# A planner that accounts for the way to SBUF shared by POOL and VectorE, and early chunks whose low parts are formed from PSUM

## The chip, the cores and the metric

The kernel runs on one core of a Trainium2 chip. The metric is the device time of one execution in microseconds (us). The five engines of the core are named as the profile names them: PE is TensorE (PEld its weight loads), DVE is VectorE, ACT is ScalarE, POOL is GpSimd, and SP issues the transfers. About 0.2% is what repeated runs of this kernel differ by.

## What is computed

A convolution-like attention over 2 x 4096 positions of width 192, followed by two feed-forward layers of inner width 2048. The first feed-forward applies h cos(h), the second a leaky ReLU.

```python
def _attn_ref(x, weight_gen):                 # (2,4096,192), (2,4096,8,7)
    w = weight_gen - np.max(weight_gen, axis=-1, keepdims=True)
    w = np.exp(w)
    w = w / (np.sum(w, axis=-1, keepdims=True) + 1e-09)
    x_pad = np.concatenate([np.zeros((B, K - 1, D), dtype=np.float32), x], axis=1)
    idx = np.arange(S)[:, None] + np.arange(K)[None, :]
    x_unf = x_pad[:, idx, :].reshape(B, S, K, H, D // H)
    return np.einsum('bshk,bskhg->bshg', w, x_unf).reshape(B, S, D)

def _moe_ref(x, w_in, w_out):                 # (8192,192), (192,2048), (2048,192)
    h = x @ w_in
    return ((h * np.cos(h)) @ w_out).astype(np.float32)

def _moe2_ref(x, w_in, w_out):
    h = x @ w_in
    return (np.maximum(0.01 * h, h) @ w_out).astype(np.float32)

def reference(**kwargs):
    x = _attn_ref(x, weight_gen).reshape(8192, 192)
    return _moe2_ref(_moe_ref(x, moe_w_in, moe_w_out), moe2_w_in, moe2_w_out)
```

The feed-forward weights arrive as 64-bit floats.

## The kernel before

**Tiles and chunks.** The 8192 tokens are cut into 16 blocks b of 512. For each layer m (0 and 1) and block, the inner width is cut into 16 pieces f of 128. One (m, b, f) is a chunk; there are 512. A chunk is five matmuls of 512 columns into a PSUM bank `h` (L645: the product is split into high and low float parts, three with the first 128 input rows, two with the remaining 64), then the activation, then the activated tile as a high part `hi` and a low part `lo`, then five matmuls that add into the block's accumulators: three with `hi` (L694 to L696) and two with `lo` (L699, L700). For m = 0 the activation is: turns on ACT (L657), angle on DVE (L664), sine on ACT (L669), product on DVE (L672), all into an SBUF tile `g`; then `hi` by a copy on ACT (or DVE) and `lo = g - hi` on POOL (L235). For m = 1 ACT applies the leaky ReLU in place in PSUM (L681) and copies `hi`, and DVE forms `lo = h - hi` from PSUM (L235).

**Streams.** Two streams of chunks alternate; the second starts six chunks later. `pos` numbers the chunks in this sequence. The first 34 contain 32 chunks of m = 0 and two of m = 1.

**Attention.** Blocks 0 and 1 form seven products of 128x768 on DVE (L461) and PE sums them through an identity (L466). Blocks 2 to 15 form products (L392, first one L385) and sums (L399, L407, L414) on DVE, all from SBUF to SBUF.

**Weights.** In the first 190 us eight groups of weights (m, g) are loaded and converted from 64-bit pieces: `size`, `low` on ACT (L564, L585), `clamp` on POOL (L567), `shift` and `merge` on DVE (L572, L578), `add` on POOL (L590), then a high copy on ACT or DVE (L230, L232) and a low subtraction on POOL (L235).

**The plan.** Nothing of the order is written by hand. Each operation is given to `Plan.op` with a due time (in chunks), a cost for each engine that may do it, what it reads and writes, and its buffers. `Plan.emit` keeps a clock for each engine, and again and again takes the operation that can start first: among those of an engine that can start within `NEAR` of the first, the one with the smallest due time. An engine other than an operation's first one is taken only where the first is busy (`ELSE`, `LEAVE`). A cost written as a tuple marks a DVE operation with SBUF operands only. Before the change such a cost is multiplied by `SHARED` = 1.55 if POOL is busy at that moment; POOL's own start doesn't depend on DVE. PE operations are held to start `SLACK` = 0.5 us after what they need, whichever engine made it.

**Buffers that matter here.** `h` takes one of three banks, `g` one of five tiles, `hi` and `lo` one of four each. A buffer comes free when its last user ends.

## Time and profile before

| | before |
|---|---|
| median of 3 runs | 1287.84 us (1287.0 to 1288.92) |
| profiled execution | 1289.18 us, its span 1287.2 us |
| PE busy in the span | 1233.0 us, 96% |
| DVE, ACT, POOL busy | 933.4 (73%), 883.4 (69%), 489.0 (38%) |
| mean granted PE clock | 0.989 of full speed |

A row's busy time includes what it waits for inside, for instance for a way to memory. PE's matmuls overlap: one row lasts about 0.39 us where a new one starts every 0.23 us, so PE's pace is read from starts and counts.

### The profile page before, as it was taken

How to read it: one execution, taken by the hardware profiler on the slowest of the kernel's cores; microseconds unless marked ns; L12 is line 12 of the kernel's file. 1: busy time of each engine (PE TensorE's matmuls, PEld its weight loads, DVE VectorE, ACT ScalarE, POOL GpSimd, SP SyncE). 2: the span in 40 equal slices, each digit the busy share in tenths (PEclk: the TensorE clock that was granted, in tenths of full speed). 3: DMA queues.
4: the chain of work that ended last, by engine and by line, in shares of the span. 5: the costliest groups of instructions: out<-in, count | busy, mean ns of one | idle time of the engine just before them, and what ended most of it. 6: DMA issues, size and time to landing. Idle time of an engine off the chain costs nothing.

```text
span 1287.2 us, 15419 instructions
## 1 busy us (share of the span) xinstructions
PE 1233.0 (96%) x5416; PEld 995.6 (77%) x5416; DVE 933.4 (73%) x1343; ACT 883.4 (69%) x1642; POOL 489.0 (38%) x398
## 2 busy tenths in 40 slices
PE   5798799999999999999999999999999999999998
PEld 4576587777778878787788878788787877888886
DVE  7998998889875776849795595866869586554333
ACT  4688776787776766767676666667676676776654
POOL 5898872566332322323323232322323232232000
...
GB/s 162 79 127 52 143 72 13 58 32 1 1 1 44 1 15 29 1 58 1 43 1 2 43 1 44 1 51 1 1 44 1 44 1 13 1 1 13 1 13 25
DMA packets 15037, 39.50 MB, mean 31 GB/s; under 512 B 1781, under 2 KB 8307, under 8 KB 14961
## 3 DMA queue, kind: packets, MB, share of 16 engines
...
q8 instruction: 42, 0.69, 0.2%
q14 instruction: 35, 0.28, 0.1%
...
## 4 chain that ended last, share of the span: by engine, by line
PE 58%; DVE 28%; ACT 7%; issue 4%; POOL 1%; DMA 1%; SPq 0%; ACTq 0%; DVEq 0%; POOLq 0%
PE h L645 29%; DVE pr L392 5%; DVE g L672 4%; DVE g L664 4%; PE acc1r L696 3%; PE acc1m L700 3%; PE acc1m L694 3%; PE acc1m L695 3%; PE acc1r L699 3%; PE acc0m L694 3%; DVE xa L399 3%; PE acc0r L696 3%; PE acc0m L695 3%; DVE lo L235 3%; PE acc0r L699 2%
## 5 line engine op out<-in xcount | busy, mean ns | idle before, releaser
L235 POOL TENSOR_TENSOR lo<-g,hi 128x512 fp32r<-128x512 f32 x256 | 358.6, 1402 | 622.1 <-ACT hi L230 552.9
L235 DVE TENSOR_TENSOR lo<-h,hi 128x512 fp32r<-128x512 f32 x256 | 175.5, 687 | 167.5 <-ACT hi L230 165.0
L669 ACT ACTIVATE g<-g 128x512 f32<-128x512 f32 x256 | 161.5, 631 | 146.5 <-DVE g L664 145.9
L672 DVE TENSOR_TENSOR g<-h,g 128x512 f32<-128x512 f32 x256 | 175.1, 687 | 82.9 <-ACT g L669 81.5
L664 DVE SCALAR_TENSOR_TENSOR g<-g,h 128x512 f32<-128x512 int32 x256 | 173.8, 681 | 56.6 <-ACT g L657 55.0
L681 ACT ACTIVATE h<-h 128x512 f32<-128x512 f32 x256 | 149.0, 582 | 86.2 <-PE h L645 85.6
L657 ACT ACTIVATE g<-h 128x512 int32<-128x512 f32 x256 | 151.2, 591 | 61.0 <-PE h L645 60.0
L230 ACT ACTIVATE hi<-g 128x512 fp32r<-128x512 f32 x242 | 152.0, 630 | 36.2 <-DVE g L672 34.2
L230 ACT ACTIVATE hi<-h 128x512 fp32r<-128x512 f32 x256 | 151.4, 592 | 6.5 <-PE acc1r L696 0.2
L694 PE MATMUL acc0m<-hi,ohi 128*128 128x512 f32 x256 | 105.0, 410 | 16.5 <-ACT hi L230 14.9
L645 PE MATMUL h<-x0hi,ihi 128*128 128x512 f32 x256 | 102.4, 400 | 4.1 <-DVE g L672 2.7
L699 PE MATMUL acc0r<-lo,or 128*128 128x512 f32 x256 | 102.4, 400 | 3.0 <-POOL lo L235 3.0
L699 PE MATMUL acc1r<-lo,or 128*128 128x512 f32 x256 | 100.6, 393 | 3.7 <-DVE lo L235 3.6
L694 PE MATMUL acc1m<-hi,ohi 128*128 128x512 f32 x256 | 102.5, 400 | 0.1
L645 PE MATMUL h<-x1hi,ihi 128*128 128x512 f32 x256 | 101.8, 398 | 0.8 <-DVE g L672 0.8
L645 PE MATMUL h<-x0rh,r 128*128 128x512 f32 x256 | 101.0, 395 | 1.1 <-ACT x0rh L230 1.1
L695 PE MATMUL acc1m<-hi,olo 128*128 128x512 f32 x256 | 100.1, 391 | 1.8 <-POOL olo L235 1.8
L645 PE MATMUL h<-x1hi,ilo 128*128 128x512 f32 x256 | 100.5, 393 | 1.4 <-POOL ilo L235 1.4
L645 PE MATMUL h<-x0lo,ihi 128*128 128x512 f32 x256 | 100.6, 393 | 0.7 <-DVE x0lo L235 0.7
L645 PE MATMUL h<-x0hi,ilo 128*128 128x512 f32 x256 | 100.8, 394 | 0.0
L645 PE MATMUL h<-x0rl,r 128*128 128x512 f32 x256 | 100.6, 393 | 0.0
L645 PE MATMUL h<-x1rl,r 128*128 128x512 f32 x256 | 100.3, 392 | 0.1
...
## 6 DMA issues: line engine op xcount, KB each, us to landing
...
```

Of the source, the lines that this page charges most:

```text
L230: nc.scalar.activation(out=out, in_=in_, func=AF.Copy)
L235: eng[e].tensor_tensor(out=out, in0=a, in1=b.bitcast(F32), op=ALU.subtract)
L645: nc.tensor.matmul(h(), w[:, c], v(), start=i == 0, stop=i == len(terms) - 1)
L657: nc.scalar.activation(out=k, in_=h(), func=AF.Copy, scale=0.5 / math.pi, bias=0.25)
L664: nc.vector.scalar_tensor_tensor(out=g(), in0=g().bitcast(I32), scalar=-2 * math.pi, in1=h(), op0=ALU.mult, op1=ALU.add)
L669: nc.scalar.activation(out=g(), in_=g(), func=AF.Sin, bias=math.pi / 2)
L672: nc.vector.tensor_tensor(out=g(), in0=h(), in1=g(), op=ALU.mult)
L681: op(pos + 0.6, {"ACT": 0.58}, lambda e: nc.scalar.activation(out=h(), in_=h(), func=AF.Prelu, alpha=0.01), [kh], [kg], [h])
L694: nc.tensor.matmul(am(), ohi[:, f % GF, :], ghi(), start=first, stop=False)
L695: nc.tensor.matmul(am(), olo[:, f % GF, :], ghi(), start=False, stop=False)
L696: nc.tensor.matmul(ar(), orr[:, f % GF, :], ghi(), start=first, stop=False)
L699: nc.tensor.matmul(ar(), orr[:, f % GF, :], glo(), start=False, stop=last)
```

## The change

1. **The planner's clock for the shared way.** A variable `port` holds the time until which either a POOL operation or a DVE operation with a tuple cost runs. Either kind may start only after it. `SHARED` goes. If a POOL and such a DVE operation could start within `YIELD` of each other, the one with the earlier due time goes.
2. **Costs.** The costs of most operations on DVE and POOL are new numbers; more DVE operations are marked as tuples.
3. **Choice and slack.** `NEAR` is 0.6 and each us of delay counts as 20 chunks of due time. What PE needs from PE itself has no slack any more; what others need from PE counts 0.06 + 0.17 us.
4. **Chunks kept in PSUM.** For odd `pos` below 34 and m = 0 the product is written back into the bank `h`; `hi` is copied from there (ACT or DVE), and `lo = h - hi` is formed by DVE instead of POOL. The bank is held until then.
5. **Offers.** Turns of m = 0, copies `hi` of m = 1, and the weights' `size` and `low` may also go to DVE.

```diff
-    HOP = 0.08
+    HOP = 0.06
     SLACK = 0.5
-    NEAR = 0.12
+    NEAR = 0.6
+    IDLE = 20.0
...
-    SHARED = 1.55
+    DRAIN = 0.17
+    YIELD = 0.01
...
-            t = max(o.ready + (self.SLACK if e == "PE" else 0.0), free[e], wire - 2.0 if e == "SP" else 0.0)
+            t = max(o.ready, free[e])
+            if e == "PE":
+                t = max(t, o.ready + self.SLACK if o.ready else 0.0)
+            else:
+                t = max(t, o.own)
...
+            if e == "POOL" or isinstance(o.cost[e], tuple):
+                t = max(t, port)
...
-                    t, _, o = min((a for a in at if a[0] <= t0 + self.NEAR), key=lambda a: a[1])
-                    if best is None or t < best[0]:
-                        best = t, e, o
+                    t, _, o = min((a for a in at if a[0] <= t0 + self.NEAR), key=lambda a: a[1] + self.IDLE * (a[0] - t0))
+                    here = t, e, o
+                    if best is None:
+                        best = here
+                    elif shared(best) and shared(here) and abs(t - best[0]) < self.YIELD:
+                        best = min(best, here, key=lambda a: a[2].due)
+                    elif t < best[0]:
+                        best = here
...
-                cost = cost[0] * (self.SHARED if free["POOL"] > t else 1.0)
+                cost = cost[0]
+                port = t + cost
+            elif e == "POOL":
+                port = t + cost
...
-                n.ready = max(n.ready, o.end + self.HOP)
+                if e == "PE":
+                    n.own = max(n.own, o.end + self.HOP + self.DRAIN)
+                else:
+                    n.ready = max(n.ready, o.end + self.HOP)
...
+    EARLY = 34
...
-                cost = (0.09 + 0.195 * n,) if e0 == "DVE" else 0.3 + 0.6 * n
+                cost = (0.12 + 0.2075 * n,) if e0 == "DVE" else 0.1 + 0.4 * n
...
+    def low_in_bank(pos):
+        return pos < EARLY and pos % 2 == 1
...
             def times(e):
-                nc.vector.tensor_tensor(out=g(), in0=h(), in1=g(), op=ALU.mult)
-
-            op(pos + 0.5, {"ACT": 0.58}, turns, [kh], [kg], [h, g])
+                nc.vector.tensor_tensor(out=h() if bank_low else g(), in0=h(), in1=g(), op=ALU.mult)
+
+            op(pos + 0.5, {"ACT": 0.58, "DVE": 0.67}, turns, [kh], [kg], [h, g])
...
-            op(pos + 1.7, {"ACT": 0.62, "DVE": (0.42,)}, lambda e: copy(e, ghi(), g()), [kg], [khi], [g, ghi])
-            op(pos + 2.0, {"POOL": 1.42}, lambda e: minus(e, glo(), g(), ghi()), [kg, khi], [klo], [g, ghi, glo])
+            if bank_low:
+                op(pos + 1.4, {"DVE": 0.67}, times, [kg], [kh], [h, g])
+                op(pos + 1.7, {"ACT": 0.585, "DVE": 0.67}, lambda e: copy(e, ghi(), h()), [kh], [khi], [h, ghi])
+                op(pos + 2.0, {"DVE": 0.67}, lambda e: minus(e, glo(), h(), ghi()), [kh, khi], [klo], [h, ghi, glo])
+            else:
+                op(pos + 1.4, {"DVE": 0.67}, times, [kh, kg], [kg], [h, g])
+                op(pos + 1.7, {"ACT": 0.63, "DVE": (0.43,)}, lambda e: copy(e, ghi(), g()), [kg], [khi], [g, ghi])
+                op(pos + 2.0, {"POOL": 1.28}, lambda e: minus(e, glo(), g(), ghi()), [kg, khi], [klo], [g, ghi, glo])
...
-            op(pos + 1.0, {"ACT": 0.58}, lambda e: copy(e, ghi(), h()), [kg], [khi], [h, ghi])
+            op(pos + 1.0, {"ACT": 0.58, "DVE": 0.67}, lambda e: copy(e, ghi(), h()), [kg], [khi], [h, ghi])
```

What the planner makes of it is read from the order of the built programs. The number behind `lo_`, `hi_` and `g_` is the chunk's `pos`; `h0_6_3` is m, b, f; the last number is only a counter.

POOL, from chunk 0's subtraction to chunk 2's, before:

```order
L235 TENSOR_TENSOR lo_0_376<-g_0_289,hi_0_362 128x512
L235 TENSOR_TENSOR ilo01_85<-wn01a_313,ihi01_84 128x512
L235 TENSOR_TENSOR olo00_82<-wn002_278,ohi00_81 128x256
L235 TENSOR_TENSOR or00_83<-wn002_278,or00_83 128x2x64
L235 TENSOR_TENSOR lo_1_410<-g_1_327,hi_1_399 128x512
L567 TENSOR_SCALAR wt012_382<-wt012_382 128x384
L590 TENSOR_TENSOR wn010_378<-wt010_352,wn010_378 128x384
L235 TENSOR_TENSOR olo01_88<-wn010_378,ohi01_87 128x256
L235 TENSOR_TENSOR or01_89<-wn010_378,or01_89 128x2x64
L235 TENSOR_TENSOR lo_2_460<-g_2_347,hi_2_447 128x512
```

and after:

```order
L263 TENSOR_TENSOR lo_0_382<-g_0_301,hi_0_344 128x512
L263 TENSOR_TENSOR ilo01_85<-wn01a_281,ihi01_84 128x512
L263 TENSOR_TENSOR olo00_82<-wn002_246,ohi00_81 128x256
L263 TENSOR_TENSOR or00_83<-wn002_246,or00_83 128x2x64
L598 TENSOR_SCALAR wt012_393<-wt012_393 128x384
L621 TENSOR_TENSOR wn010_377<-wt010_373,wn010_377 128x384
L263 TENSOR_TENSOR lo_2_484<-g_2_358,hi_2_390 128x512
```

Chunk 1's subtraction has left POOL, and chunk 2's now stands ahead of `olo01` and `or01`.

DVE at the same place, after (before, it has none of the rows with `hi_1` and `lo_1`, and the product is written to `g_1`):

```order
L708 TENSOR_TENSOR g_0_301<-h0_0_0_284,g_0_301 128x512
L609 SCALAR_TENSOR_TENSOR wt002_239<-w002_211,wt002_239 128x384
L708 TENSOR_TENSOR h0_0_1_294<-h0_0_1_294,g_1_311 128x512
L260 CAST hi_1_360<-h0_0_1_294 128x512
L698 SCALAR_TENSOR_TENSOR g_2_358<-g_2_358,h0_0_2_317 128x512
L698 SCALAR_TENSOR_TENSOR g_3_363<-g_3_363,h0_0_3_337 128x512
L489 TENSOR_TENSOR pr1_5_375<-xt1_143,smw0_134 128x768
L708 TENSOR_TENSOR g_2_358<-h0_0_2_317,g_2_358 128x512
L263 TENSOR_TENSOR lo_1_388<-h0_0_1_294,hi_1_360 128x512
```

The product of chunk 1 goes into the bank, `hi_1` is copied by DVE, and `lo_1` is formed from the bank behind a 128x768 product of attention block 1.

DVE in the later part, within attention block 7 (`pr7`, `xa7` are its products and sums), before:

```order
L672 TENSOR_TENSOR g_158_4142<-h0_6_2_4120,g_158_4142 128x512
L392 TENSOR_TENSOR pr7_3_4170<-xt7_3892,smw24_3096 128x768
L399 TENSOR_TENSOR xa7_4010<-xa7_4010,pr7_3_4170 128x768
L235 TENSOR_TENSOR lo_159_4191<-h1_3_12_4146,hi_159_4176 128x512
L664 SCALAR_TENSOR_TENSOR g_160_4189<-g_160_4189,h0_6_3_4180 128x512
L392 TENSOR_TENSOR pr7_2_4200<-xt7_3892,smw24_3096 128x768
L672 TENSOR_TENSOR g_160_4189<-h0_6_3_4180,g_160_4189 128x512
L399 TENSOR_TENSOR xa7_4010<-xa7_4010,pr7_2_4200 128x768
L235 TENSOR_TENSOR lo_161_4224<-h1_3_13_4193,hi_161_4211 128x512
L392 TENSOR_TENSOR pr7_1_4232<-xt7_3892,smw24_3096 128x768
```

and after:

```order
L708 TENSOR_TENSOR g_158_4147<-h0_6_2_4121,g_158_4147 128x512
L263 TENSOR_TENSOR lo_159_4173<-h1_3_12_4139,hi_159_4166 128x512
L420 TENSOR_TENSOR pr7_4_4183<-xt7_3886,smw24_3081 128x768
L698 SCALAR_TENSOR_TENSOR g_160_4190<-g_160_4190,h0_6_3_4177 128x512
L427 TENSOR_TENSOR xa7_4024<-xa7_4024,pr7_4_4183 128x768
L708 TENSOR_TENSOR g_160_4190<-h0_6_3_4177,g_160_4190 128x512
L263 TENSOR_TENSOR lo_161_4220<-h1_3_13_4192,hi_161_4208 128x512
L698 SCALAR_TENSOR_TENSOR g_162_4230<-g_162_4230,h0_6_4_4212 128x512
L420 TENSOR_TENSOR pr7_3_4237<-xt7_3886,smw24_3081 128x768
L708 TENSOR_TENSOR g_162_4230<-h0_6_4_4212,g_162_4230 128x512
```

Before, two wide rows stand together ahead of `lo_159`; after, at this place each wide row has a row between it and the next.

PE in the same part, from the `lo` matmuls of chunk 159 to those of chunk 160, before:

```order
L699 MATMUL acc1r_3_3725<-lo_159_4191,or13_125 128x512
L700 MATMUL acc1m_3_3722<-lo_159_4191,ohi13_123 128x512
L694 MATMUL acc0m_6_4137<-hi_160_4222,ohi00_81 128x512
L695 MATMUL acc0m_6_4137<-hi_160_4222,olo00_82 128x512
L696 MATMUL acc0r_6_4140<-hi_160_4222,or00_83 128x512
L645 MATMUL h1_3_14_4237<-x1hi3_3045,ihi13_120 128x512
L645 MATMUL h1_3_14_4237<-x1hi3_3045,ilo13_121 128x512
L645 MATMUL h1_3_14_4237<-x1lo3_3052,ihi13_120 128x512
L645 MATMUL h1_3_14_4237<-x1rh3_3048,r13_122 128x512
L645 MATMUL h1_3_14_4237<-x1rl3_3054,r13_122 128x512
L699 MATMUL acc0r_6_4140<-lo_160_4226,or00_83 128x512
L700 MATMUL acc0m_6_4137<-lo_160_4226,ohi00_81 128x512
```

and, from `h1_3_14` on, after:

```order
L679 MATMUL h1_3_14_4224<-x1hi3_3032,ihi13_120 128x512
L679 MATMUL h1_3_14_4224<-x1hi3_3032,ilo13_121 128x512
L679 MATMUL h1_3_14_4224<-x1lo3_3039,ihi13_120 128x512
L679 MATMUL h1_3_14_4224<-x1rh3_3037,r13_122 128x512
L679 MATMUL h1_3_14_4224<-x1rl3_3053,r13_122 128x512
L735 MATMUL acc0m_6_4131<-hi_160_4218,ohi00_81 128x512
L736 MATMUL acc0m_6_4131<-hi_160_4218,olo00_82 128x512
L737 MATMUL acc0r_6_4134<-hi_160_4218,or00_83 128x512
L740 MATMUL acc0r_6_4134<-lo_160_4222,or00_83 128x512
L741 MATMUL acc0m_6_4131<-lo_160_4222,ohi00_81 128x512
```

The five matmuls that stood between the `hi` and the `lo` matmuls of chunk 160 now stand ahead of both.

## Rows read from the trace of the kernel before

**Rows 1.** The page: engine totals; then groups (count | busy us, mean ns | idle, releaser).

```profile
span 1287.2 us, 15419 instructions
PE 1233.0 (96%) x5416; PEld 995.6 (77%) x5416; DVE 933.4 (73%) x1343; ACT 883.4 (69%) x1642; POOL 489.0 (38%) x398
...
L235 DVE TENSOR_TENSOR lo<-h,hi 128x512 fp32r<-128x512 f32 x256 | 175.5, 687 | 167.5 <-ACT hi L230 165.0 <-PE h L645 1.4
```

**Rows 2.** The chain that ended last, in time: start us, us, what.

```profile
1122.46 2.27 PE h L645 x10
```

**Rows 3.** Single rows in time, 20 to 40 us: start us, us, what [idle before].

```profile
21.47 1.16 PE L466 MATMUL tm<-ident,pr 128*128 128x128 f32 x8 [0.24 <-DVE pr L461]
...
23.39 0.35 DVE L572 TENSOR_SCALAR wt<-wt 128x384 int32<-128x384 int32 x1
...
23.77 0.56 DVE L578 SCALAR_TENSOR_TENSOR wt<-w,wt 128x384 int32<-128x384 int32 x1
```

**Rows 4.** Stretches: busy us (count) of PE, PEld, DVE, ACT, POOL; PEclk, DMA share, GB/s.

```profile
0.00:30.00 30.00, 14.83 (x69) 12.60 (x70) 23.15 (x34) 11.56 (x25) 15.21 (x23) 0.93 0.57 160
30.00:70.00 40.00, 32.13 (x142) 25.09 (x141) 38.14 (x51) 28.42 (x58) 34.27 (x34) 0.88 0.31 92
70.00:120.00 50.00, 48.40 (x207) 37.47 (x206) 43.98 (x60) 43.36 (x89) 45.40 (x45) 1.00 0.28 88
120.00:160.00 40.00, 31.98 (x113) 23.31 (x111) 37.37 (x51) 32.01 (x67) 34.53 (x37) 0.83 0.43 130
160.00:190.00 30.00, 28.82 (x127) 23.86 (x128) 29.20 (x38) 21.04 (x44) 23.53 (x22) 1.00 0.17 51
190.00:400.00 210.00, 204.52 (x895) 162.46 (x894) 180.24 (x256) 155.85 (x284) 93.02 (x61) 1.00 0.05 20
400.00:1250.00 850.00, 839.85 (x3727) 684.62 (x3726) 568.97 (x838) 573.17 (x1050) 243.09 (x180) 1.00 0.05 18
```

**Rows 5.** Single rows in time, 445 to 455 us, four engines.

```profile
445.00 1.88 POOL L235 TENSOR_TENSOR lo<-g,hi 128x512 fp32r<-128x512 f32 x1 [1.62 <-ACT hi L230]
...
446.24 1.46 DVE L392 TENSOR_TENSOR pr<-xt,smw 128x768 f32<-128x768 f32 x1
...
447.18 1.67 POOL L235 TENSOR_TENSOR lo<-g,hi 128x512 fp32r<-128x512 f32 x1 [0.30 <-ACT hi L230]
...
447.73 1.93 DVE L399 TENSOR_TENSOR xa<-xa,pr 128x768 f32<-128x768 f32 x1
...
449.58 0.68 DVE L235 TENSOR_TENSOR lo<-h,hi 128x512 fp32r<-128x512 f32 x1
...
450.19 0.67 DVE L664 SCALAR_TENSOR_TENSOR g<-g,h 128x512 f32<-128x512 int32 x1
...
450.78 0.94 DVE L392 TENSOR_TENSOR pr<-xt,smw 128x768 f32<-128x768 f32 x1
...
450.89 0.63 ACT L669 ACTIVATE g<-g 128x512 f32<-128x512 f32 x1 [2.62 <-DVE g L664]
...
453.21 0.50 PE L694 MATMUL acc0m<-hi,ohi 128*128 128x512 f32 x1 [0.59 <-ACT hi L230]
453.23 1.29 POOL L235 TENSOR_TENSOR lo<-g,hi 128x512 fp32r<-128x512 f32 x1 [4.39 <-ACT hi L230]
```

**Rows 6.** DVE's groups of rows in 0:190 (columns as in the page's groups).

```profile
L461 DVE TENSOR_TENSOR pr<-xt,smw 128x768 f32<-128x768 f32 x14 | 16.7, 1204 | 2.0 <-DMA xt<-in_x 1.8
L235 DVE TENSOR_TENSOR lo<-h,hi 128x512 fp32r<-128x512 f32 x22 | 14.8, 679 | 0.1
L578 DVE SCALAR_TENSOR_TENSOR wt<-w,wt 128x384 int32<-128x384 int32 x16 | 14.8, 923 | 0.2
L572 DVE TENSOR_SCALAR wt<-wt 128x384 int32<-128x384 int32 x16 | 14.3, 894 | 0.9 <-POOL wt L567 0.9
```

**Rows 7.** Single rows of POOL in time, 180 to 189 us.

```profile
187.30 1.18 POOL L235 TENSOR_TENSOR or<-wn,or 128x128 fp32r<-128x128 f32 x1
```

**Rows 8.** Waits of PE: engine, line waited for: us in total, times, longest.

```profile
PE acc0m L694 <- ACT hi L230: 14.9, 25, 2.2
```

More of the change, by code (lines that the diff above doesn't have):

```diff
@@ L41, in __init__ @@
         self.due, self.cost, self.fn, self.bufs = due, cost, fn, bufs
-        self.deps, self.next, self.ready, self.end = len(deps), [], 0.0, None
+        self.deps, self.next, self.ready, self.own, self.end = len(deps), [], 0.0, 0.0, None
         for d in deps:
@@ L85, in emit @@
         free = dict.fromkeys(("PE", "ACT", "DVE", "POOL", "SP"), 0.0)
-        wire = 0.0
+        wire = port = 0.0
         self.at = -16.0
@@ L105, in start_of, with shared @@
             return t
+        def shared(a):
+            return a[1] == "POOL" or isinstance(a[2].cost[a[1]], tuple)
         left = len(self.ops)
@@ L422, in attention @@
                 if e0 == "DVE":
-                    main, rest = (cost[0] * 0.75,), (0.36 if n == Q else 1.1,)
+                    main, rest = (cost[0] * 0.71,), (0.41,)
                 op(due + 0.4 * pace, {e0: main}, add_main, [kp, ka], [("xam", b, q0)], [xa, pr])
@@ L478, in attention_summed @@
             due = last - (K - i) * PACE[b]
-            op(due, {"DVE": (0.87,)}, product, reads, [("pr", b, k)], [xt, smw, pr])
+            op(due, {"DVE": (0.95,)}, product, reads, [("pr", b, k)], [xt, smw, pr])
             op(due + 0.5, {"PE": 0.9}, total, [("pr", b, k), "ident"] + ([("tm", b)] if i else []), [("tm", b)], [pr, tm])
@@ L486, in attention_summed @@
                     keys = keys + [("xbr", b, 0)]
-                op(due + 0.4, {"DVE": (0.36,)}, total_rest, keys, [("xbr", b, 0)], bufs)
+                op(due + 0.4, {"DVE": (0.41,)}, total_rest, keys, [("xbr", b, 0)], bufs)
             else:
@@ L510, in place @@
             op(due, {"ACT": 0.39}, lambda e, p=p, c=c: copy(e, rh()[p, c], v()[p]), [key], [("rh", m, b, i)], [rh, src])
-            op(due + 0.2, {"DVE": 0.42}, lambda e, p=p, c=c: minus(e, rl()[p, c], v()[p], rh()[p, c]),
+            op(due + 0.2, {"DVE": 0.42 if m == 0 else (0.41,)}, lambda e, p=p, c=c: minus(e, rl()[p, c], v()[p], rh()[p, c]),
                [key, ("rh", m, b, i)], [("rl", m, b, i)], [rh, rl, src])
@@ L514, in place @@
             op(due + 0.4, {"ACT": 0.39}, lambda e, p=p, p2=p2, c=c: copy(e, rh()[p2, c], v()[p]), [key], [("rh", m, b, 2 + i)], [rh, src])
-            op(due + 0.6, {"DVE": (0.35,)}, lambda e, p=p, p2=p2, c=c: copy(e, rl()[p2, c], rl()[p, c].bitcast(F32)),
+            op(due + 0.6, {"DVE": (0.29,)}, lambda e, p=p, p2=p2, c=c: copy(e, rl()[p2, c], rl()[p, c].bitcast(F32)),
                [("rl", m, b, i)], [("rl", m, b, 2 + i)], [rl])
@@ L563, in size @@
             def size(e, t=t, high=high):
+                if e == "DVE":
+                    nc.vector.tensor_single_scalar(out=t(), in_=high(), scalar=0x7FFFFFFF, op=ALU.bitwise_and)
+                    return
                 nc.scalar.activation(out=t().bitcast(F32), in_=high().bitcast(F32), func=AF.Abs)
@@ L592, in weights @@
             kt, kv = ("wt", k), ("wn", k)
-            op(due - 4.4, {"ACT": 0.18 + 0.48 * w}, size, kr, [kt], [raw, t])
-            op(due - 4, {"POOL": 0.15 + 0.65 * w}, clamp, [kt], [kt], [t])
-            op(due - 3.4, {"DVE": (0.12 + 0.45 * w,)}, shift, [kt], [kt], [t])
-            op(due - 2.8, {"DVE": (0.12 + 0.56 * w,)}, merge, [kt, *kr], [kt], [t, raw])
-            op(due - 3.2, {"ACT": 0.18 + 0.47 * w}, low, kr, [kv], [raw, v])
-            op(due - 2, {"POOL": 0.2 + 1.3 * w}, add, [kt, kv], [kv], [t, v])
+            op(due - 4.4, {"ACT": 0.18 + 0.48 * w, "DVE": (0.14 + 0.275 * w,)}, size, kr, [kt], [raw, t])
+            op(due - 4, {"POOL": 0.17 + 0.44 * w}, clamp, [kt], [kt], [t])
+            op(due - 3.4, {"DVE": (0.14 + 0.275 * w,)}, shift, [kt], [kt], [t])
+            op(due - 2.8, {"DVE": (0.16 + 0.515 * w,)}, merge, [kt, *kr], [kt], [t, raw])
+            op(due - 3.2, {"ACT": 0.18 + 0.47 * w, "DVE": (0.14 + 0.275 * w,)}, low, kr, [kv], [raw, v])
+            op(due - 2, {"POOL": 0.2 + 1.06 * w}, add, [kt, kv], [kv], [t, v])
             if i != "r":
@@ L606, in weights @@
                 for h, l, c, w2, j in cut:
-                    op(due - 1.6, {"ACT": 0.18 + 0.46 * w2, "DVE": (0.12 + 0.5 * w2,)},
+                    op(due - 1.6, {"ACT": 0.18 + 0.46 * w2, "DVE": (0.15 + 0.275 * w2,)},
                        lambda e, h=h, t=t, c=c: copy(e, h, t().bitcast(F32)[c]), [kt], [(k, "hi", j)], [t])
-                    op(due - 0.9, {"POOL": 0.3 + 1.2 * w2},
+                    op(due - 0.9, {"POOL": 0.18 + 1.1 * w2},
                        lambda e, h=h, l=l, v=v, c=c: minus(e, l, v().bitcast(F32)[c], h),
@@ L614, in weights @@
             lo = temp([P, half], "wlo", 1, f"wlo{n}", F32R)
-            op(due - 1.6, {"ACT": 0.42, "DVE": (0.4,)}, lambda e, hi=hi, t=t: copy(e, hi(), t().bitcast(F32)), [kt], [(k, "whi")], [t, hi])
-            op(due - 0.9, {"POOL": 0.85}, lambda e, hi=hi, lo=lo, v=v: minus(e, lo(), v().bitcast(F32), hi()),
+            op(due - 1.6, {"ACT": 0.42, "DVE": (0.29,)}, lambda e, hi=hi, t=t: copy(e, hi(), t().bitcast(F32)), [kt], [(k, "whi")], [t, hi])
+            op(due - 0.9, {"POOL": 0.73}, lambda e, hi=hi, lo=lo, v=v: minus(e, lo(), v().bitcast(F32), hi()),
                [kv, (k, "whi")], [(k, "wlo")], [v, hi, lo])
@@ L728, in take @@
             op(due, {"ACT": 0.62}, lambda e: copy(e, hi(), om()), [("om", m, b)], [("xhi", 1, b)], [hi, om])
-            op(due + 0.5, {"POOL": 1.35, "DVE": (0.75,)}, lambda e: minus(e, lo(), om(), hi()),
+            op(due + 0.5, {"POOL": 1.28, "DVE": (0.675,)}, lambda e: minus(e, lo(), om(), hi()),
                [("om", m, b), ("xhi", 1, b)], [("xlo", 1, b)], [lo, hi, om])
```

16 lines of the change are left out of this document (9 added, 7 removed).

## The prediction

> **What bounds the kernel now.** I read the engine totals first, then the span by stretches, then who waits for whom, then single rows in order of time. TensorE (PE) is busy 96% of the span [rows 1], but that hides three different stages. Ten matmuls issued without a gap take 2.27 us, 0.2275 each [rows 2]; eight transposes take 1.16 us with the tail of the last, about 0.11 each [rows 3]. With these two prices the counts by stretch [rows 4] show how much time PE lost in each: 30:70 holds 142 instructions, 56 of them transposes (the summing matmuls of the first attention blocks), so 86 x 0.2275 + 6 = 26 of 40 us, 14 lost; 120:160 holds 113, 26 us of 40, 14 lost; 70:120 loses 3, 160:190 1; 190:400 (36 transposes) loses 10.6 of 210; 400:1250 (132 transposes) loses 17.6 of 850. In 0:30 PE has 9 us of work, so 21 are lost, before and around the first chunk. The granted clock is 0.88 and 0.83 in the two worst stretches, after PE has waited, and 1.00 from 160 on [rows 4]: parts of them ran at the lower level, 1.2 GHz, and that is inside the 14 and 14.
>
> Up to 190 us the cause is one resource, the way to SBUF that POOL and VectorE (DVE) share. Look at the pairs in time [rows 5]: a 128x768 product alone takes 0.94 us; the one that starts at 446.24 takes 1.46 because POOL's subtraction runs until 446.88; POOL's next one takes 1.67 instead of 1.29, since that product runs until 447.70; and the addition from 447.73 takes 1.93, till POOL is through. Each waits for the whole of the other. Rows of DVE that read PSUM do not: 22 subtractions `lo<-h,hi` in 0:190 average 679 ns, beside a POOL that is busy 153 of 190 us [rows 4, 6], and 687 ns over the whole kernel [rows 1]. In 0:190 the 14 products average 1204 instead of 940 ns, and two kinds of row of the weight conversion 923 and 894 [rows 6] instead of 560 and 350 [rows 3]. Over all such groups of that stretch, each against its shortest rows, I get 44 us of waiting inside DVE's busy time and 22 inside POOL's. So by their undisturbed prices POOL has 153 - 22 = 131 us and DVE's rows with only SBUF operands have 66 us of work for one way: 197 us. (A DVE row's end overlaps the next row's start by some 0.05, as 449.58 + 0.68 against 450.19 shows [rows 5], so 197 fits into 188.) The way is hardly ever free until POOL converts the last weight block, 187.3 to 188.5 us [rows 7]. That is the bound of this stage; DVE's own work is 172 busy [rows 4] - 44 = 128.
>
> Later the way has room, and it hurts in places: two blocked attention rows from 446.24 to 449.66 hold up the angle row, ScalarE (ACT) then idles 2.62 us, and PE waits at 453.21 for `hi` [rows 5]. The like repeats in each round of some 76 us. Over the whole span PE waited 14.9 us in 25 places for it [rows 8].
>
> **The change part by part.**
>
> *Chunks kept in PSUM.* Of the first 34 chunks 16 (odd numbers with m = 0) lose their POOL subtraction: 16 x 1.29 [rows 5] = 20.6 us less on the way. In exchange DVE gets 16 x 0.69, and those read PSUM. One softmax subtraction goes to POOL early (some 0.7 us more on the way), and a few small copies leave DVE for ACT. Counted along the new order up to the last converted weight block, POOL has 112 us and DVE's SBUF rows 64.5: 176 instead of 197. At the same 188.5/197 this point comes at 169, 19.5 us earlier. DVE writing the product into PSUM appears in no row; I price it at the 0.69 of DVE's rows that read PSUM [rows 1], bounded by 0.67 (the angle row [rows 5]) and 0.94 (the wide product): 16 rows, so 4 us of DVE at the most.
>
> What is late next? DVE: 128 + 14 (16 `lo`, five `hi`, two turns, less the moved copies) = 142 us of some 163 (169 less the 6 it idles in the first ten, waiting for the first load), 87%; before, 128 of 183. ACT: 136 busy [rows 4], about 1 less now, of 169: 80%. PE needs 190 - 54 lost = 136. Nobody is full, but chunk by chunk the work passes ACT, DVE, ACT, DVE, ACT and POOL or DVE, so not all of 19.5 arrives. Bounds: 3 (DVE queues eat it) and 20 (the way remains the only limit). I take two thirds, **13 us**: at 87% DVE is fuller than POOL is now (153 of 190, 80%), so some queueing at DVE takes the place of the queue at the way. Up to the first chunk the order is nearly the same: 0.
>
> *A plan that knows the way.* It starts no POOL row beside a DVE row with SBUF operands, and prices them as the undisturbed rows (0.12 + 0.2075 x 4 = 0.95 for a product; POOL 1.28). The density of wide rows stays: between a chunk's angle row and its product stands one, behind the `lo` of the other stream often another, in both orders. What the new one lacks is the pair of wide rows in the middle of the products, with a POOL row beside each (order excerpt on DVE); one such pair stands at the end of each attention block now. So of the two or three losses of 0.3 to 0.8 us a round I count half as gone: bounds all 17.6 us, or a loss (last rival); I take **9**. In 190:400, where DVE is 86% busy (180 of 210), **6** of 10.6, bounds 0 and 9.
>
> *Work offered to ACT or DVE.* 20 turns, 44 copies `hi<-h` move from ACT to DVE over the kernel, 11 copies `hi<-g` go back: DVE about +30 us, ACT -30, mostly where DVE is at 67% (569 of 850): beside PE's work, 0; without that cover (DVE full) each turn or copy in a chunk's chain would cost PE up to its 0.69.
>
> *PE's order.* PE no longer counts half a microsecond between matmuls that depend only on PE. No instruction is added; what it may cost is the last rival. SP's transfers are the same 90 rows, and DMA share is 0.05 from 190 on: 0.
>
> Sum: 13 + 6 + 9 = 28 off the profiled execution's 1289.2 (its span, 1287.2, and 2 around it), so 1261; the median of the three runs is 1.3 below the profiled one, so **1260**.
>
> **The rivals.**
>
> *DVE eats the early gain* (0.18). A chunk kept in PSUM holds its bank of `h` until `lo` is written, at least 0.6 + 0.69 us longer, and there are three such banks. In 30:70 DVE is already 95% busy (38.1 of 40) [rows 4]. Against it: a quarter of its busy time up to 190 is waiting (44 of 172). Then 3 of 13 remain: 1270.
>
> *The moved rows gain nothing by moving* (0.07). If a DVE subtraction held the way as POOL's did, 16 x (1.29 - 0.69) = 9.6 of 20.6 would be freed and the early term would be 6: 1267. The 679 ns rows speak against it [rows 6]. The Trainium skill, Perfetto Trace Analysis, section Optimizing Scalar/DVE Operations, warns that VectorE and GpSimd share an SBUF read port, so that shifting work from one to the other might not help. By that rule it is this rival; the trace bears it out for SBUF operands only.
>
> *The plan changes rows, not waits* (0.05). Real times drift from the plan's by more than its slack, rows collide as often as now, and the early gain goes to DVE: within 0.2%, 1287.
>
> *PE comes too early to `lo`: slower* (0.10). Where five matmuls (1.14 us) stood between the `hi` and the `lo` matmuls of a chunk, now often none do (order excerpt on PE). POOL needs 1.29 us after `hi` [rows 5], the three `hi` matmuls take 0.68. If `hi` comes only just in time, as at 453.21, PE waits 0.7 us. There are 224 chunks of m = 0 after the first 32. If one in four is so, 56 x 0.7 = 39 us lost and the later gains are absent: 1289 - 13 + 39 - 1 = 1314. It decides from 40 such waits on (28/0.7). Against it: 20 matmuls, 4.55 us, still stand between a chunk's `h` and its `hi` matmul in nearly all of them, and the chain from turns to `hi` takes some 3.7 us even where `hi` comes late (0.6 for the turns, then 450.19 to 453.21 [rows 5]).
>
> **How the numbers follow.** The forecast has 0.60, the rivals 0.18, 0.07, 0.05 and 0.10. The low end takes nearly all bounds (19.5 + 9 + 17.6 = 46): 1242. The high end reaches past the first two rivals to a case where the early stage gives 3 and the later ones 5: 1280; the no-change and the slower case, 0.15, lie outside, and a little below. About 0.2% is what a measurement of this kernel can tell from no change: faster 0.60 + 0.18 + 0.07 = 0.85, same 0.05, slower 0.10.
>
> **What would show it.** Right: in 0:190 POOL busy down from 153 by more than 30, the products near 0.95 instead of 1.20; the last weight conversion at 169 to 178; the wait of `acc0m` for `hi` under 6 us in all; clock above 0.83 and 0.88 in the two early stretches. Wrong in the early term: DVE near 100% without long rows and PE waiting for DVE's `lo` or for an `h` bank. Wrong in the late term: waits of the `acc0r<-lo` matmul for POOL that recur each round. All of it falls if wide rows beside POOL's still average 1.2 us.

## The result, and the profile after

The changed kernel takes **1251.44 us** (median of 4 runs, 1251.22 to 1251.70), the kernel before 1287.51 on the same chip: ratio 0.9718, 95% interval 0.9701 to 0.9735. The forecast was 1260, with a range of 1242 to 1280: the sign and the range held, but 36 us were saved, not 28. The profiled execution has a span of 1249.5 us.

The page after, engine totals, then four of the waits of PE (us in total, times, longest):

```profile
span 1249.5 us, 15367 instructions
PE 1217.1 (97%) x5416; PEld 997.7 (80%) x5416; DVE 905.5 (72%) x1404; ACT 855.8 (68%) x1596; POOL 461.7 (37%) x383
```

```profile
PE tm L494 <- DVE pr L489: 16.8, 7, 8.5
PE acc1m L735 <- ACT hi L258: 3.9, 3, 2.0
PE acc0r L740 <- POOL lo L263: 2.7, 5, 1.3
...
PE acc0m L735 <- ACT hi L258: 0.8, 2, 0.6
```

`acc0m` waits 0.8 us for `hi` where it waited 14.9 [rows 8]; `acc1m` waits 3.9 us for it, all of it in 120:160, which the same view of before doesn't list. What is left is mostly the wait for the products of the first two attention blocks. The stretches of the kernel after, columns as in [rows 4]:

```profile
0.00:30.00 30.00, 15.51 (x66) 12.70 (x67) 22.11 (x33) 10.60 (x22) 13.77 (x21) 0.84 0.58 160
30.00:70.00 40.00, 33.49 (x147) 26.35 (x146) 35.32 (x55) 29.05 (x60) 26.96 (x30) 0.87 0.29 86
70.00:120.00 50.00, 49.17 (x212) 38.91 (x210) 46.04 (x77) 45.06 (x92) 37.53 (x41) 1.00 0.32 103
120.00:160.00 40.00, 35.34 (x142) 25.60 (x141) 35.10 (x58) 34.96 (x74) 29.04 (x35) 1.00 0.41 123
160.00:190.00 30.00, 30.00 (x137) 24.89 (x136) 24.81 (x37) 21.49 (x44) 15.09 (x16) 1.00 0.22 69
190.00:400.00 210.00, 208.91 (x936) 171.74 (x935) 177.15 (x267) 156.31 (x286) 93.15 (x64) 1.00 0.06 23
400.00:1250.00 850.00, 844.67 (x3787) 697.49 (x3785) 564.97 (x882) 558.33 (x1022) 246.16 (x177) 1.00 0.05 17
```

Read the counts of PE against [rows 4]: 120:160 holds 142 instead of 113, 190:400 936 instead of 895, 400:1250 3787 instead of 3727. 0:70 holds 213 and held 211: nothing came from there. With the prediction's prices for a matmul and a transpose, taken over every instruction from PE's first at 8.5 us on, PE lost (a few tenths of a us are the error of the two prices, so a small negative number is none):

| | 0:30 | 30:70 | 70:120 | 120:160 | 160:190 | 190:400 | 400:1200 |
|---|---|---|---|---|---|---|---|
| before | 12.8 | 14.9 | 3.5 | 15.8 | 0.1 | 11.2 | 18.4 |
| after | 13.5 | 13.8 | 2.6 | 7.6 | -0.1 | 1.8 | -0.3 |

Up to 190 us that is 47.0 before and 37.5 after, 9.5 gained; behind it 29.7 and 1.5, 28 gained. The experiments below are told in these two numbers, "early loss" and "late loss".

### The profile page after: what moved, and what is told of

Its sections match the earlier page's. It is cut to its first block, busy times and chain, and to the rows that moved or that the text cites. A ratio compares the mean times of both kernels' runs of the same rounds, so it can differ in the third digit from the quotient of the medians.

```text
span 1249.5 us, 15367 instructions
## 1 busy us (share of the span) xinstructions
PE 1217.1 (97%) x5416; PEld 997.7 (80%) x5416; DVE 905.5 (72%) x1404; ACT 855.8 (68%) x1596; POOL 461.7 (37%) x383
## 4 chain that ended last, share of the span: by engine, by line
PE 87%; DVE 5%; ACT 3%; DMA 2%; issue 1%; POOL 1%; SPq 0%; ACTq 0%; DVEq 0%; POOLq 0%
PE h L679 43%; PE acc1r L737 5%; PE acc1m L735 5%; PE acc1m L736 5%; PE acc1r L740 5%; PE acc1m L741 5%; PE acc0r L740 4%; PE acc0m L741 4%; PE acc0m L735 4%; PE acc0m L736 4%; PE acc0r L737 4%; DVE g L698 1%; DMA w00r<-in_moe_w_in 1%; DVE pr L489 1%; POOL lo L263 1%
## 5 line engine op out<-in xcount | busy, mean ns | idle before, releaser
L263 POOL TENSOR_TENSOR lo<-g,hi 128x512 fp32r<-128x512 f32 x240 | 339.0, 1414 | 582.7 <-ACT hi L258 490.6
L263 DVE TENSOR_TENSOR lo<-h,hi 128x512 fp32r<-128x512 f32 x272 | 186.4, 687 | 92.3 <-ACT hi L258 90.0
L691 ACT ACTIVATE g<-h 128x512 int32<-128x512 f32 x236 | 139.8, 595 | 132.4 <-PE h L679 131.8
L708 DVE TENSOR_TENSOR g<-h,g 128x512 f32<-128x512 f32 x240 | 164.3, 686 | 37.0 <-ACT g L703 31.6
L258 ACT ACTIVATE hi<-g 128x512 fp32r<-128x512 f32 x237 | 148.8, 629 | 49.7 <-DVE g L708 48.2
L258 ACT ACTIVATE hi<-h 128x512 fp32r<-128x512 f32 x228 | 135.4, 594 | 10.1 <-DVE h L708 1.4
L735 PE MATMUL acc0m<-hi,ohi 128*128 128x512 f32 x256 | 102.1, 399 | 0.9 <-ACT hi L258 0.8
L741 PE MATMUL acc0m<-lo,ohi 128*128 128x512 f32 x256 | 100.8, 394 | 0.0
L737 PE MATMUL acc0r<-hi,or 128*128 128x512 f32 x256 | 100.3, 392 | 0.0
L736 PE MATMUL acc0m<-hi,olo 128*128 128x512 f32 x256 | 100.2, 391 | 0.0
```

Of the source, the lines that this page charges most:

```text
L258: nc.scalar.activation(out=out, in_=in_, func=AF.Copy)
L263: eng[e].tensor_tensor(out=out, in0=a, in1=b.bitcast(F32), op=ALU.subtract)
L708: nc.vector.tensor_tensor(out=h() if bank_low else g(), in0=h(), in1=g(), op=ALU.mult)
L735: nc.tensor.matmul(am(), ohi[:, f % GF, :], ghi(), start=first, stop=False)
L736: nc.tensor.matmul(am(), olo[:, f % GF, :], ghi(), start=False, stop=False)
L737: nc.tensor.matmul(ar(), orr[:, f % GF, :], ghi(), start=first, stop=False)
```

## Experiments

The parts to tell apart are the chunks kept in PSUM, the plan's account of the way ("the clock for the way" in the expectations), the new durations, the new way to choose with the slack, and the offers. My theory: the kept chunks make the early gain, the account of the way the late one. Rivals: choice and slack, the offers, or the durations make the late one. Each ratio is to the kernel before as it ran beside that kernel, with medians of 1287.51 to 1288.46.

| kernel | median us | ratio to before, 95% interval | early loss | late loss |
|---|---|---|---|---|
| before | 1287.51 | | 47.0 | 29.7 |
| after | 1251.44 | 0.9718 (0.9701 to 0.9735) | 37.5 | 1.5 |
| after, no chunk kept | 1263.81 | 0.9806 (0.9791 to 0.9820) | 48.5 | 3.2 |
| after, no account of the way | 1268.26 | 0.9840 (0.9824 to 0.9857) | 43.0 | 13.4 |
| after, old choice and slack | 1252.80 | 0.9723 (0.9709 to 0.9738) | 37.2 | 2.6 |
| after, no offers | 1252.59 | 0.9718 (0.9704 to 0.9733) | 37.0 | 1.6 |
| after, old durations | 1262.45 | 0.9799 (0.9782 to 0.9815) | 46.7 | 3.7 |
| after, no account, old choice and slack | 1270.22 | 0.9858 (0.9843 to 0.9873) | 43.1 | 14.5 |
| before, chunks kept | 1280.10 | 0.9939 (0.9924 to 0.9953) | 38.7 | 30.0 |
| before, new durations | 1279.29 | 0.9931 (0.9916 to 0.9945) | 48.7 | 18.0 |
| after, all 32 chunks kept | 1251.80 | 0.9723 (0.9709 to 0.9736) | 36.1 | 2.4 |

**No chunk kept.**

```diff
-    EARLY = 34
+    EARLY = 0
```

> The changed kernel without the chunks kept in PSUM (EARLY 0); the plan's other rules stay. Theory (the kept chunks take work off the way that POOL and VectorE share, and that is what the first 190 us gained, 9 us of TensorE's losses): 1259 to 1264 us, the loss back mostly between 120 and 160 us, POOL's last weight conversion later than the 183.6 us of the changed kernel, POOL busy 0 to 190 us back near 145 to 153 us. Rival (the clock for the shared way gave the early gain by itself, VectorE being as long as the way in this stage): 1250 to 1254 us, TensorE's loss up to 190 us still near 38 us.

1263.81 us: 12.4 more than after, and the early loss is back at 48.5, 15.3 of it in 120:160. POOL's last weight conversion ends at 196.8 us. The theory held, but for POOL's busy time up to 190 us: 140.7 us, where it had 145 to 153.

**Kept chunks alone, on the kernel before.**

```diff
+    EARLY = 34
...
+            bank_low = low_in_bank(pos)
...
-                nc.vector.tensor_tensor(out=g(), in0=h(), in1=g(), op=ALU.mult)
+                nc.vector.tensor_tensor(out=h() if bank_low else g(), in0=h(), in1=g(), op=ALU.mult)
...
+                op(pos + 2.0, {"DVE": 0.67}, lambda e: minus(e, glo(), h(), ghi()), [kh, khi], [klo], [h, ghi, glo])
```

> The kernel of before with one thing of the change: the 16 chunks whose product and lo stay in PSUM. Theory (the kept chunks make the early gain by themselves): 1274 to 1280 us, TensorE's loss up to 190 us 36 to 40 us instead of 47.0, the loss behind 190 us as before (28 to 31 us). Rival (they need the clock for the way, which puts VectorE's and POOL's work beside each other): 1284 to 1289 us.

1280.10 us, at the edge of the theory's range: 8.4 us less than the kernel before beside it (1288.46), early loss 38.7, late loss untouched at 30.0. So the kept chunks need none of the other parts for this gain.

**All 32 chunks kept.**

```diff
-        return pos < EARLY and pos % 2 == 1
+        return pos < EARLY
```

> The changed kernel with twice the dose: all 32 of the first 34 chunks that belong to the first expert layer stay in PSUM, instead of 16 of them; POOL gives 16 more lo of 1.28 us to VectorE (0.68 us each, with the 0.26 us by which hi on VectorE or product grow where they move). Theory (with 16 kept the way is no longer what sets the last weight conversion, VectorE is, so 11 us more for VectorE before 190 us is no gain): 1251 to 1258 us, POOL busy below 106 us up to 190 us and still idle for VectorE's wt, TensorE's loss from 70 to 160 us 10 to 16 us (10.2 in the changed kernel). Rival (the way is still what the stage waits for, so that the second 16 give what the first gave, less what is left to give): 1243 to 1248 us, that loss 3 to 6 us.

No gain. The stage 0:190, of the kernel after and of this one:

```profile
0.00:190.00 190.00, 163.52 (x697) 128.45 (x698) 163.39 (x256) 141.16 (x288) 122.38 (x142) 0.95 0.36 108
```

```profile
0.00:190.00 190.00, 160.26 (x703) 126.45 (x704) 167.38 (x274) 140.99 (x289) 100.67 (x126) 0.96 0.36 107
```

POOL (the fifth pair) falls by 22 us, and PE does 703 instructions instead of 697 in the 190 us. POOL's last conversion ends at 183.6 us in both. The first 16 chunks had already taken POOL's load off the limit. Part of my expectation missed: I had the loss between 70 and 160 us at 10 to 16, it is 9.7; VectorE took the added 4 us without harm.

**No account of the way.**

```diff
+    SHARED = 1.55
...
-            if e == "POOL" or isinstance(o.cost[e], tuple):
-                t = max(t, port)
...
-                    elif shared(best) and shared(here) and abs(t - best[0]) < self.YIELD:
-                        best = min(best, here, key=lambda a: a[2].due)
...
-                cost = cost[0]
-                port = t + cost
-            elif e == "POOL":
-                port = t + cost
+                cost = cost[0] * (self.SHARED if free["POOL"] > t else 1.0)
```

> The changed kernel whose plan no longer keeps VectorE's SBUF-only instructions and POOL's apart: no clock for the way, no yielding, and the factor 1.55 of before on VectorE's SBUF-only costs while POOL is at work; costs, choice rule, kept chunks and offers stay. Theory (the clock is what removed the 27 us after 190 us): 1272 to 1280 us, 190 to 400 us losing 8 to 12 us again and the rounds behind 400 us 14 to 20 us. Rival (the choice rule and the slack did it): 1251 to 1256 us, with the losses behind 190 us under 6 us.

1268.26: the theory had 1272 to 1280, the rival 1251 to 1256; both missed. The late loss comes back to 13.4, not to 29.7, and 5.5 us of the early gain go too. So I looked for what holds the other 16.

**Old choice and slack.**

```diff
-    HOP = 0.06
+    HOP = 0.08
...
-    NEAR = 0.6
-    IDLE = 20.0
+    NEAR = 0.12
...
-                    n.own = max(n.own, o.end + self.HOP + self.DRAIN)
+                    n.ready = max(n.ready, o.end + self.HOP)
```

> The changed kernel with the old way to choose: among the instructions that can start within 0.12 us the one with the earliest due time (before: 0.6 us, at a price of 20 due steps for each us), the slack and the hop counted behind TensorE's results as behind the others', hop 0.08. The clock for the way, the new costs, the kept chunks and the offers stay. Theory (the clock removed the 27 us behind 190 us): 1250 to 1257 us. Rival (choice and slack removed them): 1268 to 1280 us, the rounds behind 400 us losing 12 us or more.

The second run takes out the account of the way as well.

> The changed kernel with neither the clock for the way nor the new choice rule and slack: the durations, kept chunks and offers are what is left of the change. Theory (choice and slack are worth nothing with or without the clock): 1266 to 1271 us, as without the clock alone. Rival (they are worth something only where the clock is missing): 1276 to 1284 us, with the losses behind 190 us back above 22 us.

With the account 1252.80, without it 1270.22 against 1268.26: both intervals overlap those of their partners, and both theories held. Choice and slack are worth nothing that these runs can tell.

**No offers.** The weights' `size` and `low` go back to ACT alone too.

```diff
...
-            op(pos + 0.5, {"ACT": 0.58, "DVE": 0.67}, turns, [kh], [kg], [h, g])
+            op(pos + 0.5, {"ACT": 0.58}, turns, [kh], [kg], [h, g])
...
-            op(pos + 1.0, {"ACT": 0.58, "DVE": 0.67}, lambda e: copy(e, ghi(), h()), [kg], [khi], [h, ghi])
+            op(pos + 1.0, {"ACT": 0.58}, lambda e: copy(e, ghi(), h()), [kg], [khi], [h, ghi])
```

> The changed kernel without the new offers: turns and hi of the second expert layer's chunks on ScalarE alone, size and low of the weight conversions on ScalarE alone. Theory (the offers are worth nothing, as the sum of the prediction has them): 1250 to 1253 us. Rival (the 64 instructions that VectorE takes from ScalarE are part of the late gain): 1257 to 1270 us, with TensorE waiting for ScalarE's hi behind 400 us again, some 15 us as before the change.

1252.59, the same ratio as after. The offers are worth nothing that can be measured.

**The durations.** First the new ones alone on the kernel before, then the old ones in the kernel after; one of some twenty lines:

```diff
-            op(due, {"DVE": (0.87,)}, product, reads, [("pr", b, k)], [xt, smw, pr])
+            op(due, {"DVE": (0.95,)}, product, reads, [("pr", b, k)], [xt, smw, pr])
```

> The kernel of before with one thing of the change: the new durations of instructions in the plan (the factor 1.55 on VectorE's SBUF-only work beside POOL stays, no offers, no kept chunks). Theory (the durations are what the run without the clock kept of the late gain, 16 us of 28): 1270 to 1277 us, the loss behind 190 us 12 to 18 us instead of 29.7. Rival (the durations are worth little, the choice rule and the slack kept those 16 us): 1283 to 1289 us.

> The changed kernel with the durations of before in its plan; clock for the way, choice rule, slack, kept chunks and offers stay. Theory (with the clock the plan needs the new durations too, since those of before are up to 50% too long for POOL's and VectorE's conversion steps): 1258 to 1268 us, most of it lost up to 190 us, 4 to 10 us behind it. Rival (the clock alone carries it): 1250 to 1255 us.

Alone, the durations take the late loss from 29.7 to 18.0, but the early loss rises by 1.7, and 1279.29 us lies between the two ranges. With the account of the way but the durations of before the late loss is 3.7, and 1262.45 us is where the theory had it. So for the late gain the account hardly needs the durations, and they do nearly half of it where the account is missing (11.7 of 28.2 us on the kernel before); the two overlap. The account was not put into the kernel before by itself, but of the parts that every run with it also has, choice, offers and kept chunks, none made a late gain in a run of its own. In the early stage the account needs true durations: with the old ones the loss is 46.7, as if no chunk were kept.

How the account works is in the groups of DVE and POOL between 400 and 1250 us (count | busy, mean ns). The kernel before:

```profile
L392 DVE TENSOR_TENSOR pr<-xt,smw 128x768 f32<-128x768 f32 x54 | 62.5, 1158 | 0.3
```

```profile
L235 POOL TENSOR_TENSOR lo<-g,hi 128x512 fp32r<-128x512 f32 x167 | 226.1, 1354 | 505.9 <-ACT hi L230 453.0 <-PE acc1m L700 41.4 <-issue 4.5
```

Before with the new durations, and after without the account:

```profile
L392 DVE TENSOR_TENSOR pr<-xt,smw 128x768 f32<-128x768 f32 x54 | 65.5, 1212 | 0.2
```

```profile
L414 DVE TENSOR_TENSOR pr<-xt,smw 128x768 f32<-128x768 f32 x54 | 68.9, 1276 | 0.0
```

The kernel after:

```profile
L420 DVE TENSOR_TENSOR pr<-xt,smw 128x768 f32<-128x768 f32 x53 | 50.3, 948 | 0.0
```

```profile
L263 POOL TENSOR_TENSOR lo<-g,hi 128x512 fp32r<-128x512 f32 x164 | 229.2, 1398 | 467.9 <-ACT hi L258 391.7 <-PE acc1m L741 31.4 <-issue 29.9
```

With the account the products take their undisturbed 0.95 us (948 to 968 ns in every run that has it), without it 1.16 to 1.28. But POOL's rows got longer, 1398 against 1354 ns. POOL's rows and VectorE's wide rows still meet; now it is POOL that waits, and POOL stood idle for 468 us of this stretch. That POOL waits is not needed for the gain: with the old choice and slack, where the account stays, POOL's rows got shorter as well, and the late loss is 2.6:

```profile
L255 POOL TENSOR_TENSOR lo<-g,hi 128x512 fp32r<-128x512 f32 x164 | 217.4, 1326 | 481.0 <-ACT hi L250 425.6 <-DVE hi L252 27.6 <-PE acc1m L733 15.4
```

What all runs with the account share is that VectorE's wide rows are not held up. Single rows of the kernel after, 428 to 439 us (compare [rows 5]):

```profile
428.00 0.94 DVE L420 TENSOR_TENSOR pr<-xt,smw 128x768 f32<-128x768 f32 x1
...
428.28 1.82 POOL L263 TENSOR_TENSOR lo<-g,hi 128x512 fp32r<-128x512 f32 x1 [2.22 <-ACT hi L258]
...
429.95 0.96 DVE L427 TENSOR_TENSOR xa<-xa,pr 128x768 f32<-128x768 f32 x1
...
436.74 0.95 DVE L427 TENSOR_TENSOR xa<-xa,pr 128x768 f32<-128x768 f32 x1
...
436.96 1.88 POOL L263 TENSOR_TENSOR lo<-g,hi 128x512 fp32r<-128x512 f32 x1 [3.21 <-ACT hi L258]
```

The product starts first and has the way; POOL's row, 0.28 us later, lasts 1.82 instead of 1.29; the addition comes when POOL is just through (428.28 + 1.82 = 430.10) and takes 0.96. The length of the wide rows is not the whole of the late loss, though: the durations alone took 12 us off it with products no shorter (1212 ns). What went is PE's wait for `hi`. Between 190 and 1240 us, before and before with the new durations:

```profile
PE acc0m L694 <- ACT hi L230: 9.7, 21, 0.6
```

```profile
PE acc0m L694 <- ACT hi L230: 1.9, 3, 0.9
```

Why the new durations bring `hi` in time is not settled; it isn't by shorter wide rows.

**Why the first 70 us gained nothing.** Two kernels leave out work of nearly the same length, one on POOL, one on VectorE, in an untouched order.

```diff
             def clamp(e, t=t):
+                if early:
+                    return
...
             def add(e, t=t, v=v):
+                if early:
+                    return
```

> The changed kernel, its plan and order untouched, without POOL's clamp and POOL's sum of high and low half for the weights of the first three groups of the first expert layer (22 instructions, 18.3 us of POOL's 40.7 between 0 and 70 us); those weights are wrong by that. It asks why the first 70 us gained nothing. Theory (VectorE's own work is the bound there, since POOL's load on the shared way already fell by 9 us without a gain): 1248 to 1252 us, TensorE's loss up to 70 us still 25 to 28 us (27.3 in the changed kernel). Rival (the way that both share is still the bound): 1238 to 1245 us, that loss 14 to 20 us.

```diff
             def shift(e, t=t):
+                if early:
+                    return
...
             def merge(e, t=t, high=high):
+                if early:
+                    return
...
-            def total_rest(e, pr=pr, old=old):
+            def total_rest(e, pr=pr, old=old, i=i):
+                if i > 1:
+                    return
```

> The changed kernel, its plan and order untouched, without VectorE's shift and merge for the weights of the first three groups of the first expert layer and without the last five of six sums of the 64 columns behind column 128 in the first two blocks of tokens (28 instructions, 17.6 us of VectorE's 57.4 between 0 and 70 us); weights and those columns are wrong by that. Theory (VectorE's own work is the bound there): 1238 to 1245 us, TensorE's loss up to 70 us 14 to 20 us. Rival (the shared way): the same, but then the run without POOL's 18 us gives as much. Third (neither, but steps that follow one on the other between engines and loads): 1248 to 1252 us in both.

Without POOL's 18.3 us: 1247.86 (0.9685, 0.9671 to 0.9700), 22.2 us lost up to 70 us instead of 27.3. Without VectorE's 17.6 us: 1243.75 (0.9654, 0.9638 to 0.9670), 19.5 lost. The stage 0:70 of after, without POOL's work, and without VectorE's:

```profile
0.00:70.00 70.00, 49.01 (x211) 39.06 (x212) 57.44 (x87) 39.64 (x82) 40.73 (x51) 0.85 0.42 118
```

```profile
0.00:70.00 70.00, 48.57 (x232) 38.54 (x233) 56.97 (x96) 44.02 (x91) 25.74 (x33) 0.93 0.42 119
```

```profile
0.00:70.00 70.00, 53.05 (x245) 44.02 (x246) 47.58 (x66) 46.51 (x97) 45.51 (x59) 0.90 0.48 134
```

VectorE's work counts for more than POOL's, 7.7 us against 3.6 by the medians (7.8 against 5.1 by the loss up to 70 us), but neither theory holds alone: POOL's was expected to give nothing, VectorE's run ended inside its range, and more than half of the 27 us stays in both. VectorE's rows that were left out also used the way, so how much of the 7.7 us is VectorE's own time and how much the way is open. What stays, the first loads and a chain of single steps up to the first chunk among it, was not tried.

**Does the low clock cost anything there?** Between 20 and 35 us the granted clock is 0.54, so most of it is at the lower of the two levels, after PE had stood idle from 15.8 to 19.9. I filled PE's pauses with matmuls that add zeros.

```diff
+    FILL = {(0, 5): 14, (0, 6): 3, (1, 1): 8}
...
+    zeros = const.tile([P, P], F32, name="zeros")
...
             def total(e, i=i, pr=pr):
+                for _ in range(FILL.get((b, i), 0)):
+                    nc.tensor.matmul(tm()[:, :P], ident, zeros, start=False, stop=False)
```

> The changed kernel with 25 more matmuls of 128x128 (zeros, added to tm, so that no result changes) where TensorE stands idle in the first 40 us: 14 ahead of the sixth tap of block 0, 3 ahead of the seventh, 8 ahead of the second tap of block 1. Theory (the granted clock of 0.5 to 0.6 between 20 and 34 us follows TensorE's pause of 4.1 us ahead of 19.9 us, and costs 5 to 6 us of matmul time there, of which VectorE's pace lets half through): clock 1.00 from 20 to 34 us, TensorE's loss up to 70 us 3 us smaller beside the 6 us that the added matmuls fill, 1247 to 1250 us. Rival (VectorE sets the pace there whatever the clock): the clock is 1.00 and the time stays at 1251 to 1252 us, with longer waits for VectorE's products in place of the slow matmuls. Third (the pause is not what lowers the clock): clock still 0.5 to 0.6 after 20 us.

20:35 of the kernel after, then of this one, and single rows on PE, two of the kernel after and three of this one (each added matmul leaves two rows, so the 14 stand as x28):

```profile
20.00:35.00 15.00, 13.18 (x42) 9.86 (x43) 11.91 (x21) 8.36 (x19) 6.62 (x9) 0.54 0.21 66
```

```profile
20.00:35.00 15.00, 10.13 (x50) 6.80 (x50) 12.81 (x22) 9.89 (x22) 7.49 (x10) 1.00 0.28 88
```

```profile
25.24 0.79 PE L679 MATMUL h<-x0hi,ihi 128*128 128x512 f32 x1 [0.26 <-ACT x0hi L258]
...
34.70 0.50 PE L679 MATMUL h<-x0hi,ihi 128*128 128x512 f32 x1
```

```profile
16.05 3.29 PE L497 MATMUL tm<-zeros,ident 128*128 128x128 f32 x28
...
23.59 0.50 PE L684 MATMUL h<-x0hi,ihi 128*128 128x512 f32 x1 [0.31 <-ACT x0hi L259]
...
33.05 0.50 PE L684 MATMUL h<-x0hi,ihi 128*128 128x512 f32 x1 [2.34 <-DVE g L713]
```

The clock is 1.00 and the first chunk starts at 23.59 us, 1.65 earlier than in the kernel after, where a matmul row then takes 0.79 us instead of 0.50. The faster matmuls add to this lead, until PE waits 2.34 us for VectorE's `g` at 33.05, where it had not waited before (34.70): what the clock had added is given back, and the lead is 1.65 again. It shrinks further behind, and from 150 us on the same matmul starts 0.2 us earlier than in the kernel after. 1250.83 us, 0.9708 (0.9693 to 0.9722): within the intervals the same as after. The rival held.

No kernel here beats the changed one by more than the intervals show, apart from the two that leave work out.

## Why the prediction was right, and where its steps were off

*The bound up to 190 us.* POOL's rows were the limit of the worst stretch: moving 16 of them to VectorE and PSUM, and nothing else, took 120:160 from 15.8 to 9.9 us lost on the kernel before. Whether they were the limit as load on the way, as the prediction has it, or as POOL's own queue (34.5 of these 40 us busy [rows 4]) no run separates, since a moved row leaves both. For 0:70 the way was not shown to be the limit: VectorE's products of the first two blocks still take 1275 ns (1204 before [rows 6]). By the prediction's own sign ("wide rows beside POOL's still average 1.2 us") the account failed there: it did not keep the two engines apart, and why was not tried. Groups of DVE in 0:190 of the kernel after:

```profile
L489 DVE TENSOR_TENSOR pr<-xt,smw 128x768 f32<-128x768 f32 x14 | 17.7, 1275 | 1.5 <-DMA xt<-in_x 1.4
L708 DVE TENSOR_TENSOR h<-h,g 128x512 f32<-128x512 f32 x16 | 11.1, 694 | 2.5 <-ACT g L703 2.3
L708 DVE TENSOR_TENSOR g<-h,g 128x512 f32<-128x512 f32 x16 | 10.9, 681 | 0.5 <-ACT g L703 0.3
L609 DVE SCALAR_TENSOR_TENSOR wt<-w,wt 128x384 int32<-128x384 int32 x16 | 10.0, 627 | 0.1
L603 DVE TENSOR_SCALAR wt<-wt 128x384 int32<-128x384 int32 x16 | 9.0, 563 | 0.0
```

*The early term, 13.* Near: 11.0 by taking the kept chunks away (12.4 in the medians), 9.5 between the two traces. The price of a product into PSUM, 0.69, is the measured 694 ns. The step that failed is the end of the stage, put at 169 to 178 us. POOL's last conversion and its `wn` rows (idle 18.8 us for VectorE), kernel after:

```profile
183.12 0.46 POOL L263 TENSOR_TENSOR or<-wn,or 128x128 fp32r<-128x128 f32 x1
```

```profile
L621 POOL TENSOR_TENSOR wn<-wt,wn 128x384 int32<-128x384 int32 x16 | 18.4, 1152 | 18.8 <-DVE wt L609 18.8
```

It ends at 183.6, 4.9 earlier than [rows 7], not 19.5. The sum of the way fell as counted (POOL 122 us busy instead of 153, the mark of "more than 30" just met), but after that POOL waits for VectorE's `wt`: what I listed as late next came sooner than I gave it, and 32 kept chunks show that the way then has room to spare. The kept chunks by themselves moved this end by 7.8 us on the kernel before (188.5 to 180.7) and by 13.2 in the kernel after (196.8 to 183.6); the rest of the change put it 8.3 later. And PE lost nothing in 160:190 in either kernel (0.1 and -0.1), so the last conversion is not what it waited for. That two thirds of 19.5 came near what was gained is therefore partly luck. The marks on the clock came half true: 1.00 for 0.83 in 120:160, 0.87 for 0.88 in 30:70.

*The late terms, 6 and 9.* Both mis-sized: they measure 9.4 and 18.7, a little above their upper bounds of 9 and 17.6. The step that failed is "I count half as gone", argued from wide rows that stay as dense as they were. They stay, and in the kernel after they still meet POOL's. But the account of the way orders them so that VectorE's row comes first or just after, and in the kernel after it is POOL that waits. POOL can wait: it is 29% busy there (246 of 850), and PE's waits for its `lo` did not come. The sum 13 + 6 + 9 = 28 measures 9.5 + 9.4 + 18.7 = 37.6, the difference of the two profiled spans (37.7); the medians differ by 36.1.

*Offers 0, PE's order 0.* Both right within the noise, by the run without the offers and the one with the old choice and slack.

*The rivals.* That DVE eats the early gain: no, 9.5 of it came. That the rows moved to VectorE gain nothing by moving: no, though not by the time alone, since the 8.4 us of the kept chunks on the kernel before lie between this rival's 6 and the forecast's 13. The moved rows show it: VectorE's subtractions from PSUM keep their 683 ns (41 rows in 0:190), those into the bank take 694. That was also what the Trainium skill's caution against shifting work between GpSimd and VectorE (Perfetto Trace Analysis, section Optimizing Scalar/DVE Operations) would have made of it; the trace disagrees for rows that read PSUM. That PE comes too early to `lo`: no, `acc0r` waited 2.7 us in 5 places. That the plan changes rows and not waits: no, the late loss went from 29.7 to 1.5.

The Trainium skill, SBUF — State Buffer, section Who interferes with whom, says that the order of issue decides which of the two engines blocks, for the whole instruction. The trace agrees (POOL's 1.88 at 436.96, VectorE's 1.93 at 447.73 in [rows 5]); I had read it for whether they collide, not for which of them has time to wait.
